# Two FFN chunks of batch 0 queued later, the first k and q of batch 1 and the transposes of batch 2 ahead of other loads

## The chip, the cores and the metric

The kernel runs on one core of a Trainium2 chip. The metric is the device time of one execution in microseconds (us); the median of several is compared. A core has a matrix engine (PE, with its weight loads listed as PEld), a vector engine (DVE), an engine for activation functions (ACT), a general one (POOL) and a synchronisation engine (SP). Each works through its own instructions in the order in which the program gives them. An instruction whose data is not there holds up all that stands behind it on its engine. Loads and stores are issued by POOL, SP or ACT and are then carried out by 16 DMA engines, while the issuing engine goes on.

## What is computed

Sigmoid attention for 8 batches of 12 heads, followed by a gated feed-forward network (FFN) over all 3584 tokens. All inputs are float32; the kernel converts them to float16 as it loads them.

```python
S = q.shape[2]                                   # 448; heads are 64 wide
scores = np.matmul(q, k.transpose(0, 1, 3, 2)) / sqrt(64) - np.log(S)
attn = 1.0 / (1.0 + np.exp(-scores))
x = np.matmul(attn, v)                           # then heads side by side: (3584, 768)
out = (np.maximum(x @ w_gate, 0) * (x @ w_val)) @ w_out   # 768 -> 1536 -> 768
```

## The kernel before

**The pieces.** A batch has 12 heads, worked in three groups of four (`NG = 3`; groups 0, 1, 2). For a group, k and q must first be transposed, so that the head dimension lies on partitions. For batches 0 and 1 PE does it (`pe_transposes`, L201: one call for k and one for q, into a PSUM tile `trt`, which DVE copies to `qkT`, L206). From batch 2 on DVE reorders k and q into `rel` (L215) and SP issues a DMA transpose (`dma_transposes`, L219). A group then has seven score units (`qk_unit`, L232: matmuls into two PSUM banks, then two sigmoids by ACT, L187), and after its seventh one product with v (`pv`, L250), whose result DVE scales into `xT` (L184).

**The FFN** works in 12 chunks of 128 columns of the gate and value weights. A chunk (`gv`, L309) is six matmuls for the gate into `g_ps` and six for the value into `v_ps`; then the gate's maximum with 0 by DVE (L320) or ACT (L318, where `act_relu` is true), and the product by DVE into `hT` (L327). Later batches, and batches 2 and 3 in part, use another form of the products with sums of weights (L393), which the change does not touch; `weight_sums` (L384) are DVE's sums over `wo` for it.

**Batch 0** is special. Its queries are cut in two halves of 256 and 192 (`HALVES`), and the work in six slots (`FirstSlot`: half by half, group by group) of four units each. A unit of two score chunks takes one of two double banks (`pairp`), so a third unit needs the sigmoid of the first. The table `after` says what PE does after unit u of slot i: transposes, products with v of earlier slots, or FFN chunks. Its FFN chunks come in two kinds: wide ones for the first half (256 columns) and narrow ones for the second (192), 12 of each.

**The FFN queue.** `push_first` and `push_gv` put chunks into `gv_queue`, and `ffn_mix(count, hooks)` takes `count` of them out, in order. A hook `(left, job)` runs its job when `left` chunks of the mix are still to come. Batch 1's scores come in six bursts of 3, 3, 3, 4, 4 and 4 units (`cuts`), and each burst is followed by a mix of so many chunks (`mix`). The hooks put into the mixes what must be ready for later bursts: PE transposes of batch 1's groups 1 and 2, and the DMA transposes of batch 2.

**The order of loads.** POOL issues all loads into one queue. Before anything else it has batch 0's k, q and v, the gate and value weights in pieces (`load_gv(f0, f1)`: chunks f0 to f1, the gate's piece `wg`, then the value's `wv`), and batch 1's k, q (by group) and v in between. The issues of k and q are L110, of v L114 and L116, of weights L148, of `wo` L164. In the first mix of batch 1 it gets batch 2's loads. `hold(b, g)` is a tiny POOL copy (L735) that reads a transposed tile: POOL, and so every load behind it, waits until that DMA transpose has landed. `late_loads` issues batch 2's last transposes, a hold, and the loads of `wo`; batch 3's k, q and v follow (they are issued in batch 2's first mix).

**PSUM banks.** During the slots four banks rotate (`ring0`) beside the two double banks. After the slots these become four more (`ring1`), and eight rotate (`bank`).

Of the kernel before, what the change touches and what calls it, by code (L numbers as in the profile page):

```python
# [17 lines left out]
def kernel(  # L18
# [84 lines left out]
    def rows_of(src, b):  # L103
        return src[b].rearrange("(x r) (t c) d -> (r t) x (c d)", r=2, c=NCH)

    def load(b, g0, g1, which, c0=0, c1=NCH):
        for nm, t16, src in zip("kq", tiles_of(b), (k, q)):
            if nm in which:
                xs, cs = slice(2 * g0, 2 * g1), slice(c0 * D, c1 * D)
                nc.gpsimd.dma_start(t16[:, xs, cs], rows_of(src, b)[:, xs, cs])  # L110

    def load_v(b):
        v16 = tiles_of(b)[2]
        nc.gpsimd.dma_start(v16[:, 0::2, :], rows_of(v, b)[:, 0::2, :])  # L114
        for r in range(2):
            nc.gpsimd.dma_start(  # L116
                v16[64 - 64 * r : P - 64 * r, 1::2, :], rows_of(v, b)[64 * r : 64 * r + 64, 1::2, :]
            )
# [25 lines left out]
    def load_gv(f0, f1, which=(0, 1)):  # L144
        fs = slice(f0 * P, f1 * P)
        for i in which:
            wt, src = ((wg, moe_w_gate), (wv, moe_w_val))[i]
            nc.gpsimd.dma_start(wt[:, :, fs], src[:, fs].rearrange("(c p) f -> p c f", p=P))  # L148
# [2 lines left out]
    load(0, 1, NG, "q", QCUT)  # L151
    load_gv(0, 2, (1,))
    load_gv(2, 4)
    load_gv(4, 6)
    load(1, 0, 1, "kq")
    load_gv(6, 9)
    load(1, 1, 2, "kq")
    load_v(1)
# [36 lines left out]
    def pe_transposes(b, g, ti, c0=0, c1=NCH):  # L195
        t16 = in_tiles[b][ti]
        qkT = qkT_of(b, g)
        trt = bank16("trt")
        for c in range(c0, c1):
            for h in range(2):  # L200
                nc.tensor.transpose(  # L201
                    trt[64 * h : 64 * h + 64, c * P : (c + 1) * P],
                    t16[:, 2 * g + h, c * D : (c + 1) * D],
                    ident[:],
                )
        nc.vector.tensor_copy(  # L206
            qkT[:, ti * NCH + c0 : ti * NCH + c1, :].rearrange("p c x -> p (c x)"),
            trt[:, c0 * P : c1 * P],
        )

    def dma_transposes(b, g):
        k16, q16, _ = in_tiles[b]
        rel = relp.tile([P, TW, P], FP16, tag="rel", name="rel")
        for ti, t16 in enumerate((k16, q16)):
            nc.vector.tensor_copy(  # L215
                rel[:, ti * NCH : (ti + 1) * NCH, :].rearrange("p c (h d) -> p h c d", h=2),
                t16[:, 2 * g : 2 * g + 2, :].rearrange("p h (c d) -> p h c d", c=NCH),
            )
        nc.sync.dma_start_transpose(  # L219
            qkT_of(b, g)[:], rel[:].rearrange("p c x -> p (c x)")  # L220
        )
# [433 lines left out]
    def push_first(half, fs, act_relu=True):  # L655
        c0, c1 = HALVES[half]
        push_gv(0, 64 * c0, 64 * (c1 - c0), fs, act_relu)

    def ffn_mix(count, hooks=()):
        hooks = list(hooks)  # L660
        for left in range(count, -1, -1):
            while hooks and hooks[0][0] >= left:
                hooks.pop(0)[1]()
            if left:
                gv_queue.popleft()()
# [8 lines left out]
    pe_transposes(0, 0, 1, 0, QCUT)  # L674
    keep_warm(2)
    slots = [FirstSlot(half * NG + g, g, half) for half in range(2) for g in range(NG)]
    push_first(0, range(0, 6), False)
    def second_queries():
        for g in range(1, NG):
            pe_transposes(0, g, 1, QCUT, NCH)  # L680

    def pv_then_ffn(i):
        slots[i].pv()
        ffn_mix(1)

    def ffn_then_pv(i):
        ffn_mix(1)
# [18 lines left out]
        (3, 3): lambda: ffn_mix(1),  # L706
        (4, 1): lambda: ffn_then_pv(3),
        (4, 3): lambda: ffn_mix(2),
        (5, 1): lambda: pv_then_ffn(4),
        (5, 3): lambda: ffn_mix(1),  # L710
    }
    for i, slot in enumerate(slots):
        for u in range(4):
# [1 line left out]
            if (i, u) in after:  # L715
                after[(i, u)]()
    slots[5].pv()
    push_first(1, range(0, 6))
    for f0 in range(6, 12, 2):
        for half in range(2):  # L720
            push_first(half, range(f0, f0 + 2))

# [11 lines left out]
    def hold(b, g):  # L734
        nc.gpsimd.tensor_copy(gate[0:1, :], qkT_tiles[(b, g)][0:1, 0, 0:2])  # L735

    def both(b, g):
        pe_transposes(b, g, 0)
        pe_transposes(b, g, 1)

    def late_loads():
        dma_transposes(2, 2)
        hold(2, 1)
        load_o()


# [38 lines left out]
            prepare()  # L785
            down(g, i)

    ffn_mix(1, [(1, lambda: both(1, 0))])
    for b in range(1, B):
        if b == 1:  # L790
            cuts, pv_at = (0, 3, 6, 9, 13, 17, 21), {3: (0, 2), 5: (1, 2)}
        else:
            cuts, pv_at = (0, 4, 7, 11, 14, 18, 21), {0: (-1, 2), 2: (0, 2), 4: (1, 2)}
        bursts = list(range(len(cuts) - 1))
        inner = {}
        if b > 2:
            inner = {0: 1} if b % 2 == 0 else {2: 3, 3: 5} if b == B - 1 else {4: 5}
            for n in inner.values():
                bursts.remove(n)
        count = len(bursts)  # L800
        hooks = {}
        if b == 1:
            mix = (3, 3, 3, 3, 3, 2)
            hooks = {
                1: [(1, lambda: both(1, 1))],
                3: [(1, lambda: both(1, 2))],
                4: [(3, lambda: dma_transposes(2, 0))],
                5: [(2, lambda: dma_transposes(2, 1)), (0, late_loads)],
            }
        elif b == 2:  # L810
            mix = (2, 2, 1, 1, 1, 2)
            hooks = {
                2: [(0, prepare)],
                4: [(0, lambda: weight_sums(0))],
                5: [(1, lambda: weight_sums(1)), (0, lambda: weight_sums(2))],
            }
            open_late()
        elif b == 3:
            mix = (1, 1, 1, 0, 0)
        else:  # L820
            mix = (0,) * count

        def burst(n):
            for i, (g, c) in enumerate(order[cuts[n] : cuts[n + 1]]):
                if n in pv_at and i == pv_at[n][1]:
                    if n == 0:
                        pv_finish(b - 1)
                        if b == 2:
                            push_group(0)
                        elif b % 2 == 0:  # L830
                            push_group(b // 2 - 1)
                    else:
                        pv_group(b, pv_at[n][0])
                qk_unit(b, g, c)

        if b == 3:
            dma_transposes(3, 2)
            for args in put_off:
                stored(*args)
        for m in range(count):  # L840
            jobs = []
            burst(bursts[m])
            if m == 0 and b > 3:
                jobs.append(lambda: dma_transposes(b, 2))
            if b == 2 and m == count - 1:
                jobs.append(lambda: (dma_transposes(3, 0), dma_transposes(3, 1)))
            elif b == 3 and m == count - 1:
                jobs.append(lambda: dma_transposes(4, 1))
            elif 0 <= m - count + 2 and 3 < b < B - 1:
                jobs.append(lambda: dma_transposes(b + 1, m - count + 2))  # L850
            if b == 1:
                if m == 0:
                    load(2, 0, 1, "kq")
                    load(2, 1, 2, "kq")
                    load(2, 2, 3, "kq")
                    load_v(2)
            elif m == 0 and b + 1 < B:
                if b == 3:
                    jobs.append(lambda: hold(3, 2))
                jobs.append(lambda: (load(b + 1, 0, 3, "kq"), load_v(b + 1)))  # L860
            if b % 2 and b > 2:
                if m == count - 1:
                    jobs.append(lambda: (batch_sums_t1(b // 2), batch_sums(b // 2, (0, 1))))
            elif b > 3 and m == 0:
                jobs.append(lambda: batch_sums(b // 2 - 1, (1, HD)))
            if b == 2 and m == count - 1:
                ffn_mix(mix[m], hooks[m])
                next_work(jobs + [lambda: weight_sums(3)], first_act=True)
            elif mix[m]:
                for job in jobs:  # L870
                    job()
                ffn_mix(mix[m], hooks.get(m, ()))
            else:
                next_work(jobs, amid=(lambda: burst(inner[m])) if m in inner else None)
            if b == 3 and m == count - 2:
                dma_transposes(4, 0)
            if b == 3 and m in (1, 3):
                for f in range(*((0, 8, 2), (8, NFC, 2))[m // 2]):
                    gate_sums(f, f + 2)
# [35 lines left out]
```

## Time and profile before

| | |
|---|---|
| median of three runs | 392.95 us (392.91 to 393.34) |
| the profiled execution | 392.75 us, of which 391.0 us from its first to its last instruction |
| granted TensorE clock | 0.998 |
| slots of batch 0 | up to about 31 us |
| bursts of batch 1 | 33.57 to 60.4 us, the first of batch 2 at 62.46 us |
| POOL held by batch 2's hold | until 67.76 us |
| read from HBM, written | 47.19 MB, 11.01 MB |

In the profile, L393 is line 393 of the code; `out<-in` gives the tiles that an instruction writes and reads. A line of a timeline has the start in us, the time from the first start to the last end of the instructions that it sums up, the engine, the line, the operation and how many there are; in brackets stands how long the engine was idle before it, and what ended that. Matmuls overlap, so two groups that follow each other closely can overlap by some 0.1 us on paper: the distance from start to start is what a group costs. An answer by tile lists instructions with their shortest, median and longest duration in ns, the start of the first and the last in us, and for loads the time from issue to landing.

### The profile page before, as it was taken

The numbers are of one execution on the slowest core, as the hardware profiler recorded it, in microseconds if no ns is written. First come the engines' busy times: TensorE is split into PE (matmuls) and PEld (weight loads), VectorE is DVE, ScalarE is ACT, GpSimd is POOL, SyncE is SP. The second block draws the span as 40 slices with busy tenths as digits, with TensorE's granted clock in tenths as the row PEclk, the third lists the DMA queues.
The fourth block names the chain that finished last, engine by engine and source line by source line (L and its number), as shares of the span: only waits on it lengthen the run. The fifth ranks groups of instructions, "written<-read, shape, count | busy, mean of one in ns | idle before, by whom it ended". The sixth has DMA issues, their size and how long they took to land.

```text
span 391.0 us, 8760 instructions
## 1 busy us (share of the span) xinstructions
PE 384.2 (98%) x3488; PEld 214.8 (55%) x3488; DVE 283.5 (73%) x557; ACT 226.9 (58%) x480; POOL 49.5 (13%) x73
## 2 busy tenths in 40 slices
PE   8999999999999999999999999999999999999996
PEld 3678786445455545454555554545455555555663
DVE  2454344358387789999757789999987788999663
ACT  5946778784777755555556774545467354333322
POOL 8633420500300300003000300000000000000000
PEclk9999999999999999999999999999999999999999
DMA  9999999998999892225956595132002320000335
GB/s 149 197 199 204 204 204 138 145 202 148 191 185 167 156 217 44 47 49 64 179 99 137 114 222 86 21 49 59 18 14 73 78 80 2 0 1 2 78 87 159
DMA packets 68953, 43.69 MB, mean 112 GB/s; under 512 B 35888, under 2 KB 65584, under 8 KB 68912
## 3 DMA queue, kind: packets, MB, share of 16 engines
q0 software_dynamic: 30736, 23.33, 39.8%
q1 hardware_dynamic: 37664, 19.24, 24.3%
q10 hardware_dynamic: 512, 0.56, 0.5%
q8 instruction: 27, 0.44, 0.5%
q14 instruction: 14, 0.11, 0.1%
HBM read 47.19 MB, written 11.01 MB: 149 GB/s over the span
## 4 chain that ended last, share of the span: by engine, by line
PE 90%; DMA 5%; POOL 1%; DVE 1%; ACT 1%; issue 0%; POOLq 0%; DVEq 0%; ACTq 0%
PE u L393 33%; PE g L393 16%; PE y L393 10%; PE qk_ps L232 8%; PE pv_ps L250 7%; PE g_ps L309 7%; PE v_ps L309 6%; DMA wv<-in_moe_w_val_dram 4%; DMA v<-in_v_dram 2%; PE ya L354 1%; PE trt L201 1%; PE yb L354 1%; POOL k L110 1%; POOL q L110 1%; ACT PT L187 1%
## 5 line engine op out<-in xcount | busy, mean ns | idle before, releaser
L187 ACT ACTIVATE PT<-qk_ps 128x448 f16<-128x448 f32 (+3 forms) x318 | 150.8, 585 | 76.2 <-PE qk_ps L232 76.1
L393 PEld LDWEIGHTS <-S 128*128 128x128 f16 x558 | 54.6, 98 | 44.7
L605 DVE TENSOR_TENSOR gsb<-g,gsb 128x448 f32<-128x448 f32 x72 | 42.8, 625 | 10.3 <-PE g L393 10.0
L232 PE MATMUL qk_ps<-qkT 64*64 64x448 f16 (+2 forms) x756 | 47.4, 335 | 0.8 <-DVE qkT L206 0.5
L327 DVE TENSOR_TENSOR hT<-gate_sb,v_ps 128x256 f16<-128x256 f32 (+2 forms) x36 | 16.2, 465 | 35.2 <-ACT gate_sb L318 18.0
L393 PEld LDWEIGHTS <-hT 128*128 128x128 f16 x306 | 28.7, 98 | 22.3 <-issue 4.9
L601 ACT COPY gsb<-u 128x448 f32<-128x448 f32 x48 | 25.6, 558 | 24.0 <-PE u L393 22.9
L445 ACT ACTIVATE ysb<-u 128x384 f32<-128x384 f32 x31 | 15.2, 491 | 38.2 <-PE u L393 33.8
L250 PE MATMUL pv_ps<-PT,v 64*64 64x448 f16 (+2 forms) x756 | 36.6, 329 | 0.0
L184 DVE TENSOR_SCALAR xT<-pv_ps 128x448 f16<-128x448 f32 (+2 forms) x53 | 27.9, 567 | 11.9 <-PE pv_ps L250 10.8
L309 PE MATMUL v_ps<-xT,wv 128*128 128x256 f16 (+2 forms) x216 | 33.3, 290 | 0.4 <-DMA wv<-in_moe_w_val_dram 0.4
L309 PE MATMUL g_ps<-xT,wg 128*128 128x256 f16 (+2 forms) x216 | 33.5, 291 | 0.1
L393 PEld LDWEIGHTS <-wg 128*128 128x128 f16 x216 | 20.2, 98 | 21.8 <-issue 4.3
L393 PEld LDWEIGHTS <-wv 128*128 128x128 f16 x216 | 21.1, 98 | 19.7
L232 PEld LDWEIGHTS <-qkT 64*64 64x64 f16 x756 | 17.9, 105 | 22.0 <-issue 14.7
L463 DVE SCALAR_TENSOR_TENSOR ysb<-y,ysb 128x384 f32<-128x384 f32 x29 | 16.1, 556 | 17.9 <-PE y L393 10.4
L250 PEld LDWEIGHTS <-v 64*64 64x64 f16 x756 | 21.7, 107 | 10.8 <-issue 0.9
L393 PE MATMUL u<-T,hT 128*128 128x384 f16 x132 | 25.1, 326 | 0.0
L110 POOL DMA_DIRECT2D k<-in_k_dram x14 | 10.9, 776 | 112.4 <-DVE rel L215 105.7
L309 PEld LDWEIGHTS <-wg 128*128 128x128 f16 x216 | 18.5, 98 | 11.7 <-issue 5.1
L309 PEld LDWEIGHTS <-wv 128*128 128x128 f16 x216 | 20.1, 98 | 8.1 <-DMA wv<-in_moe_w_val_dram 0.7
L393 PE MATMUL u<-xT,wg 128*128 128x448 f16 x108 | 23.5, 354 | 0.0
(76 smaller groups left out, 531.2 us busy)
## 6 DMA issues: line engine op xcount, KB each, us to landing
out_dram<-ysb SPq DMA_DIRECT2D x52, 192.0 KB, 2.8
k<-in_k_dram POOLq DMA_DIRECT2D x5, 672.0 KB, 11.4
q<-in_q_dram POOLq DMA_DIRECT2D x5, 672.0 KB, 14.7
v<-in_v_dram POOLq DMA_DIRECT2D x8, 336.0 KB, 14.9
v<-in_v_dram POOLq DMA_DIRECT2D x16, 168.0 KB, 13.8
k<-in_k_dram POOLq DMA_DIRECT2D x8, 224.0 KB, 11.9
wo<-in_moe_w_out_dram POOLq DMA_DIRECT2D x1, 1536.0 KB, 11.1
q<-in_q_dram POOLq DMA_DIRECT2D x6, 224.0 KB, 12.1
```

The lines of the kernel that those rows point to most:

```text
L110: nc.gpsimd.dma_start(t16[:, xs, cs], rows_of(src, b)[:, xs, cs])
L184: nc.vector.tensor_scalar(out=xT, in0=src, scalar1=XSCALE, scalar2=None, op0=AOP.mult)
L187: nc.scalar.activation(PT_ap, ps_ap, AF.Sigmoid, bias=sig_bias, scale=qk_scale)
L232: nc.tensor.matmul(out_of(hh)[o : o + 64, :], qkT[rows, c, cols], qkT[rows, NCH + c0 : NCH + c1, cols], start=True, stop=True, tile_positi ...
L250: nc.tensor.matmul(ps[hh][64 * r : 64 * r + 64, 0:qn], v16[rows, 2 * g + hh, c * D : (c + 1) * D], pieces[c][rows, hh, :], start=(c == 0), ...
L309: nc.tensor.matmul(ps[-1][:, 0:qn], wt[:, dc, f * P : (f + 1) * P], xT_tiles[b][:, dc, q0 : q0 + qn], start=(dc == 0), stop=(dc == NDC - 1),)
L327: nc.vector.tensor_tensor(out=hT_tiles[g][:, f, o : o + qn], in0=gate_sb[:, 0:qn], in1=ps[1][:, 0:qn], op=AOP.mult,)
L393: nc.tensor.matmul(ps[:, 0:n], A[:, k_, :], W[:, k_, :], start=(first and k_ == 0), stop=(k_ == kn - 1), skip_group_check=True,)
L445: nc.scalar.activation(o, ps[:, 0:HM], AF.Copy, scale=OUT_SCALE)
L463: nc.vector.scalar_tensor_tensor(out=o, in0=ps[:, 0:HM], scalar=OUT_SCALE, in1=o, op0=AOP.mult, op1=AOP.add)
L601: by(gs[u][i][:], ps[u][:, 0:S])
L605: nc.vector.tensor_tensor(out=gs[u][i][:], in0=ps[u][:, 0:S], in1=gs[u][i][:], op=AOP.add)
```

## The change

Four things change.

1. Batch 1's k and q of group 0 are issued ahead of the weights of chunks 4 and 5.
2. Chunks 4 and 5 of batch 0's first half leave the slots. They are now queued behind four narrow chunks, so that the order in the queue is 0 to 3 narrow, 4 and 5 wide, 4 and 5 narrow, 6 and 7 wide, and so on, where it was 0 to 5 narrow, 6 and 7 wide, 6 and 7 narrow, and so on. The queue has 20 chunks instead of 18. The two chunks get their gate by ACT and not by DVE.
3. Batch 1's first transposes go into slot 5, behind its third unit, and the single chunk between the slots and batch 1's first burst goes: the burst follows slot 5's product with v. The mixes of batch 1 become 4, 3, 3, 3, 3, 4, after one chunk ahead of them and 3, 3, 3, 3, 3, 2.
4. Batch 2's DMA transposes of group 1 go from the last mix of batch 1 into the fifth, with one chunk to come; those of group 2 go from the end of the last mix to behind its first chunk. POOL holds for group 2 instead of group 1, and batch 2's v is loaded behind that hold and ahead of `wo`; it was loaded ahead of the hold, behind batch 2's k and q.

```diff
@@ -151,8 +151,8 @@
     load_gv(2, 4)
+    load(1, 0, 1, "kq")
     load_gv(4, 6)
-    load(1, 0, 1, "kq")
     load_gv(6, 9)
@@ -674,14 +674,10 @@
-    push_first(0, range(0, 6), False)
+    push_first(0, range(0, 4), False)
...
-    def pv_then_ffn(i):
-        slots[i].pv()
-        ffn_mix(1)
@@ -706,8 +702,8 @@
-        (5, 1): lambda: pv_then_ffn(4),
-        (5, 3): lambda: ffn_mix(1),
+        (5, 1): slots[4].pv,
+        (5, 2): lambda: (pe_transposes(1, 0, 0), pe_transposes(1, 0, 1)),
@@ -715,8 +711,8 @@
     slots[5].pv()
-    push_first(1, range(0, 6))
-    for f0 in range(6, 12, 2):
+    push_first(1, range(0, 4))
+    for f0 in range(4, 12, 2):
@@ -740,7 +736,8 @@
     def late_loads():
         dma_transposes(2, 2)
-        hold(2, 1)
+        hold(2, 2)
+        load_v(2)
         load_o()
@@ -785,7 +782,6 @@
-    ffn_mix(1, [(1, lambda: both(1, 0))])
@@ -800,12 +796,12 @@
-            mix = (3, 3, 3, 3, 3, 2)
+            mix = (4, 3, 3, 3, 3, 4)
             hooks = {
                 1: [(1, lambda: both(1, 1))],
                 3: [(1, lambda: both(1, 2))],
-                4: [(3, lambda: dma_transposes(2, 0))],
-                5: [(2, lambda: dma_transposes(2, 1)), (0, late_loads)],
+                4: [(3, lambda: dma_transposes(2, 0)), (1, lambda: dma_transposes(2, 1))],
+                5: [(3, late_loads)],
             }
@@ -853,7 +849,6 @@
                     load(2, 2, 3, "kq")
-                    load_v(2)
```

## Prediction

> **What bounds the kernel now.** I read the page first, then TensorE's timeline (PE) of the first 110 us, the answers by tile for the loads, and last the DVE, ACT, POOL and SP timelines there.
>
> ```profile
> PE 384.2 (98%) x3488; PEld 214.8 (55%) x3488; DVE 283.5 (73%) x557; ACT 226.9 (58%) x480; POOL 49.5 (13%) x73
> DMA  9999999998999892225956595132002320000335
> GB/s 149 197 199 204 204 204 138 145 202 148 191 185 167 156 217 44 47 49 64 179 99 137 114 222 86 21 49 59 18 14 73 78 80 2 0 1 2 78 87 159
> ```
>
> PE is busy for 384.2 of 391.0 us, and the change takes no matmul away: it can only move PE's gaps. The rates say where a gap can arise: slices are 9.8 us, and until about 58 us the transfers run flat at some 200 GB/s, one queue, in the order written. In that stretch a load lands when the bytes ahead of it are through, however early PE wants it.
>
> ```profile
> 27.05 0.83 PE L309 MATMUL g_ps<-xT,wg 128*128 128x256 f16 x6
> 28.32 0.83 PE L309 MATMUL v_ps<-xT,wv 128*128 128x256 f16 x6 [0.45 <-DMA wv<-in_moe_w_val_dram]
> 38.03 0.67 PE L309 MATMUL g_ps<-xT,wg 128*128 128x192 f16 x6
> 38.53 0.66 PE L309 MATMUL v_ps<-xT,wv 128*128 128x192 f16 x6
> ...
> 40.53 0.56 PE L201 MATMUL trt<-ident,q 128*64 128x128 f16 x14
> ...
> 48.73 0.83 PE L309 MATMUL g_ps<-xT,wg 128*128 128x256 f16 x6
> 49.39 0.82 PE L309 MATMUL v_ps<-xT,wv 128*128 128x256 f16 x6
> ...
> 51.87 0.56 PE L201 MATMUL trt<-ident,q 128*64 128x128 f16 x14
> ```
>
> From start to start, half an FFN chunk costs 0.66 us when wide (256 columns, batch 0's first half) and 0.50 when narrow (192, the second half): 1.32 and 0.99 a chunk. The v half at 28.32 follows its g half by 1.27, so PE loses 0.61 there, waiting for the weights of chunk 4. The two transposes of q (L201) at 40.53 and 51.87 wait for nothing. How long had their data been there? POOL's loads of q for batch 1's groups 1 and 2:
>
> ```profile
> L110 POOL DMA_DIRECT2D q<-in_q_dram x1: 713/713/713, 23.9 to 23.9; - x1
> DMA to landing us min/median/max: 14.6/14.6/14.6
> ```
>
> ```profile
> L110 POOL DMA_DIRECT2D q<-in_q_dram x1: 713/713/713, 37.7 to 37.7; - x1
> DMA to landing us min/median/max: 12.3/12.3/12.3
> ```
>
> By POOL's timeline they start at 23.93 and 37.68, so they land at 38.5 and 50.0: 2.0 and 1.9 us before PE wants them. These two slacks decide the change.
>
> **The change, part by part.**
>
> *Loads.* Batch 1's first k and q (224 KB each, 1.1 us each in the stream) go ahead of the weights of chunks 4 and 5. They now land at 29.3 and 30.5; they will land near 24.8 and 25.9, and those weights at 30.5 instead of 28.3. Everything behind them lands when it did: the bytes ahead are the same.
>
> *Slot 5 and the first burst.* Out of the stretch from 26.0 go three FFN chunks, two wide and one narrow. With them go the 0.61 stall and three changes between FFN and scores, about 0.1 each (the v half before the scores of 29.08 takes 0.76, not 0.66). What comes in: slot 5's four sigmoids (1.51 and 1.19 us of ACT, now with PE's wait between) run on end, and PE has less to put beside them. Unit 2 needs unit 0's bank: ready at 26.48 + 0.76 and a hand-over, so 27.4, where PE arrives at 27.05; with some 0.15 before the last probabilities of the last pv, 0.5. Bounds: 0, if the transposes fill it, and 0.9, if the whole last pv and the burst stand behind ACT's end (26.48 + 2.70 + 0.70 + 0.69 = 30.6, against 29.7 of PE's own work from 26.0). The early balance is thus 0 to 0.9 us gained, likeliest 0.4. DVE's gate (0.42, L320) becomes ACT's (0.38, L318) for two chunks; ACT idles 4.8 of the 20 us from 34 to 54, so this costs nothing; without that room it would be 0.8.
>
> *The trap.* The moved chunks are work that stood ahead of the transposes and now stands behind them. At group 1's transposes PE has done two narrow chunks less than before (chunks 4 and 5 of the second half): it comes 4 x 0.50 = 2.0 earlier, besides the early gain. Slack 2.0: any early gain is waited away here, and PE leaves level with before. At group 2's it has done two wide chunks less (8 and 9 of the first half): 4 x 0.66 = 2.63 earlier, slack 51.87 - 49.98 = 1.89, and 0.05 from landing to start. **PE waits 0.79 us for q.** No later work returns it: the skipped chunks all come in mixes 4 and 5, and at batch 2's first burst PE has done the same as before, at 63.2 instead of 62.46. Bounds: 0.5 and 1.1, from one transfer's scatter in the same stream (a step of 1.12 or 1.15 us for 224 KB, but 2.7 for 384 KB where 1.9 is usual).
>
> *Batch 2's transposes.* Those of group 1 go up into mix 4 and of group 2 into mix 5 behind one chunk. Their six DVE copies (0.39 each) and SP's three transposes are the same. Group 2's copies stand behind the product of that chunk (about 60.6, since ACT ends eight sigmoids first), so SP issues it at about 61.7. It took 5.3 to 5.8 us there: group 2 lands at 66 to 67.5. Group 0's is needed at 63.2 and issued near 53; even at its 7.4 of now it is there.
>
> *v and wo.* POOL's hold moves from group 1 (released at 67.76) to group 2 (66 to 67.5), and behind it now stand three loads of v, two of wo, and batch 3's k, q and v. From hold to first issue is 1.1 us now (67.76 to 68.83); the wo that came first took 11.1 for 1536 KB, of which 9.4 is bytes at the rate of the second (768 KB in 4.7), so a start costs 1.7. v (672 KB, 3.4 us) then lands by 74; its first pv comes at 75.06 + 0.8 = 75.9. wo ends near 86 to 88, wanted by DVE at 87.61 + 0.8. Both costed at nothing, with 1 to 2 us of cover; without it, each microsecond late at v is one on PE. POOL gains 2.0 us of issues here; PE and DVE don't wait for POOL.
>
> *Batch 3's first transposes.* This is what is late next. Batch 3's v now lands last at 73.86 + 20.8 = 94.7, and SP starts group 0's transposes at 94.97, on empty queues; PE takes them up the moment they land:
>
> ```profile
> L219 SPq DMA_TRANSPOSE qkT<-rel x1: 1510/1510/1510, 95.0 to 95.0; - x1
> DMA to landing us min/median/max: 4.1/4.1/4.1
> ```
>
> ```profile
> 99.12 0.14 PEld L232 LDWEIGHTS <-qkT 64*64 64x64 f16 x8 [0.38 <-DMA qkT<-rel]
> ```
>
> After: v's 3.4 us more, less 0.2 to 1.8 from the earlier hold: the loads end at 96.3 to 97.9, SP starts at 95.77. So they overlap by 0.5 to 2.1. What overlap costs:
>
> ```profile
> L219 SPq DMA_TRANSPOSE qkT<-rel x1: 3106/3106/3106, 54.7 to 54.7; - x1
> DMA to landing us min/median/max: 7.4/7.4/7.4
> ```
>
> That one had 5.9 us of loads beside it (until 60.55) and took 3.3 longer, 0.56 per us. This gives 0.3 to 1.2; I take 0.5, since its data moves only about 1 us after the issue. Bounds: nothing (the loads are out first) and 1.6 (SP's issue alone went from 1.51 to 3.11).
>
> The Trainium skill ("DMA: Bandwidth & Descriptors", Queues, rings and completion order) says that each DMA engine goes round between the queues that have work, packet by packet. That both queues move at once is what the row of 54.7 shows too. By the rule a transpose beside a load gets half of each engine and is held up by half of the true overlap: an estimate from that page of 0 to 0.5 us, and a sum of 393.54 to 394.04. The row is a little dearer, and the sum stays with the row.
>
> The skill also has a rule that speaks for the change: "Mode switching requires drain" ("TensorEngine Tiling (Array Packing)", Key Properties). It names no price; the trace agrees with about 0.1 us each. By the rule the early stretch gains three of them, and the sum is the same, since the gain is waited away at group 1's transposes.
>
> **Sum.** The profiled execution took 392.75 us (span 391.0 and 1.75 around it): 392.75 + 0 (early gain, lost) + 0.79 (q of group 2) + 0.5 (batch 3's transposes) = 394.05. The median shown is 392.95, 0.2 above that execution, so I forecast **394.2**. A change under 0.2% (0.79 us) can't be told from none here.
>
> **Rivals.**
> 1. *The q is late and nothing else*, or late by less: 392.95 + 0 to 0.79, up to 393.74. For it: batch 3's loads may end before SP's data moves. Against: the stall at 99.12 shows no cover there.
> 2. *v or wo takes over.* v is late if the hold is released after 69.4 (75.9 less 1.1, 1.7, 3.4 and 0.3). Group 2's landing is 63.75 + 5.3 = 69.06 now, for a copy 2 us later in the program, so this is near. Price 1 to 3 us: 395.3 to 397.
> 3. *Faster.* The loads keep pace: q of group 2 must land by 49.2 (0.8 earlier) and of group 1 at 38.1. Then the 0.61 stall and the switches are saved: 0.4 to 0.8, so 392.15 to 392.5. It decides only if those landings move; against it speak the flat 200 GB/s and unchanged bytes ahead of both. A stream 2% faster would do it for group 2.
>
> **Chances.** The forecast (q late, batch 3's transposes somewhat late, 393.5 to 395.3) 0.62; rival 1: 0.16; rival 2: 0.12; rival 3: 0.10. Above 393.74 lie most of the forecast (0.58) and rival 2: slower 0.70. Within 0.2%: rival 1 and 0.04 of the forecast, 0.20. Faster 0.10. The range 392.9 to 395.9 leaves out rival 3 and the far end of rival 2.
>
> **What would show it.** The 0.61 stall at chunk 4's v half is gone. PE waits for DMA q at group 1's transposes (about 38.5) and 0.8 us at group 2's (about 50.0), both named. Batch 2's first burst starts near 63.2, hold ends at 66 to 67.5, v lands before 75, and the wait at batch 3's first scores has grown to 0.5 to 1.5 over 0.38. The prediction is wrong if q of group 2 lands before 49.3, if pv of batch 2 waits for v, or if PE makes up time between 63 and 99 us.

## The result and the profile after

| | before | after |
|---|---|---|
| median of 21 runs each | 393.09 us (392.46 to 394.21) | 393.97 us (393.47 to 395.11) |
| the profiled execution | 392.75 us, span 391.0 | 394.54 us, span 392.7 |

The ratio is 1.0022, with a 95% interval of 1.0016 to 1.0029: **0.88 us slower**. The profiled execution of after lies 0.57 above its median, and that of before 0.34 below its own, so the two traces differ by 1.8 us where the kernels differ by 0.9. What is not typical is named below. Bursts and mixes of batch 1 are numbered from 0 to 5 here, as in the code.

The page of the changed kernel, its busy time of engines and its transfers in 40 slices:

```profile
PE 385.2 (98%) x3488; PEld 215.8 (55%) x3488; DVE 282.4 (72%) x555; ACT 227.8 (58%) x482; POOL 49.4 (13%) x73
...
DMA  9999995998999793224956595042103320000335
GB/s 152 198 199 205 203 176 93 195 203 149 198 173 172 143 214 66 47 48 48 170 107 142 114 216 99 12 52 56 26 7 76 82 80 2 0 1 2 78 88 157
```

The stream still runs at 200 GB/s until batch 2's k and q are in. The slices from 49 to 69 us have become emptier (176 and 93 for 204 and 138), since v now waits for the hold. PE's timeline of the changed kernel, in the stretch that the change rewrites:

```profile
27.47 0.36 PE L232 MATMUL qk_ps<-qkT 64*64 64x192 f16 x8 [0.23 <-ACT PT L187]
...
28.86 0.33 PE L201 MATMUL trt<-ident,q 128*64 128x128 f16 x5 [0.24 <-issue]
...
30.05 0.28 PE L250 MATMUL pv_ps<-PT,v 64*64 64x192 f16 x4 [0.16 <-ACT PT L187]
...
38.72 0.56 PE L201 MATMUL trt<-ident,q 128*64 128x128 f16 x14
...
49.00 0.58 PE L201 MATMUL trt<-ident,k 128*64 128x128 f16 x14
49.81 0.58 PE L201 MATMUL trt<-ident,q 128*64 128x128 f16 x14 [0.23 <-DMA q<-in_q_dram]
...
56.14 0.79 PE L232 MATMUL qk_ps<-qkT 64*64 64x448 f16 x8
56.56 1.77 PE L250 MATMUL pv_ps<-PT,v 64*64 64x448 f16 x28
57.98 0.72 PE L232 MATMUL qk_ps<-qkT 64*64 64x448 f16 x8
58.63 0.83 PE L309 MATMUL g_ps<-xT,wg 128*128 128x256 f16 x6
...
63.34 0.57 PE L232 MATMUL qk_ps<-qkT 64*64 64x448 f16 x8
```

Chunk 4's stall on its weights is gone. In its place stand two short waits for ACT in slot 5, a wait for q at group 2's transposes, and a burst 5 whose pieces take longer on paper (before, its pv took 1.49). The wait at 49.81 is longer than its bracket, because the transposes of k beside it are drawn overlapping: k's start at 49.00 and cost 0.42 before, so PE was free at 49.42 and lost 0.39. The load of that q, by its answer by tile:

```profile
L110 POOL DMA_DIRECT2D q<-in_q_dram x1: 713/713/713, 36.8 to 36.8; - x1
...
DMA to landing us min/median/max: 13.0/13.0/13.0
```

It lands at 49.77 (before: 49.98), and PE starts at 49.81.

To see where time comes in, I set both traces' PE instructions of the same work side by side; from batch 2's first burst on their order is the same. The changed kernel is behind by 0.12 us when the two programs first differ (at 26.0; scatter of the first loads), by 0.18 at the first chunk after batch 1's first burst, by 0.61 after group 2's transposes, by 0.88 at batch 2's first burst (63.34 against 62.46), and still by 0.86 at batch 3's first scores. That is close to the difference of the medians. The trace then loses another 0.79 at 121.9, which belongs to this execution:

```profile
118.95 0.39 DVE L215 COPY rel<-q 128x896 f16<-128x896 f16 x1 [1.22 <-DMA q<-in_q_dram]
...
121.86 1.14 PE L393 MATMUL u<-T,S 128*128 128x384 f16 x6 [0.63 <-DVE ysb L440]
```

DVE waits for batch 4's q, whose load took 12.6 us here and 11.3 before. None of the nine experiments' traces has this step.

### The profile page after: what moved, and what is told of

Read it like the earlier page. It is cut to its first block, busy times and chain, and to the rows that moved or that the text cites. A ratio compares the mean times of both kernels' runs of the same rounds, so it can differ in the third digit from the quotient of the medians.

```text
span 392.7 us, 8755 instructions
## 1 busy us (share of the span) xinstructions
PE 385.2 (98%) x3488; PEld 215.8 (55%) x3488; DVE 282.4 (72%) x555; ACT 227.8 (58%) x482; POOL 49.4 (13%) x73
## 4 chain that ended last, share of the span: by engine, by line
PE 81%; DMA 13%; POOL 2%; DVE 2%; issue 1%; ACT 0%; POOLq 0%; DVEq 0%; ACTq 0%
PE u L393 33%; PE g L393 16%; PE y L393 10%; PE qk_ps L232 7%; DMA q<-in_q_dram 7%; PE pv_ps L250 6%; PE g_ps L309 4%; PE v_ps L309 4%; DMA k<-in_k_dram 4%; DMA wg<-in_moe_w_gate_dram 3%; POOL q L110 1%; PE ya L354 1%; POOL k L110 1%; ACT PT L187 0%; PE yb L354 0%
```

## The experiments

The theory at the start: the loss is the wait for q at group 2, and the part on batch 2 costs nothing. The rivals: the late v and wo cost it, or slot 5 under ACT's pace does. Times are medians; "before" is run beside each group (393.05, 393.19 and 392.95).

| run | us | ratio to before, 95% interval |
|---|---|---|
| e1_front_only | 394.26 | 1.0040 (1.0028 to 1.0052) |
| e2_back_only | 393.18 | 1.0008 (0.9999 to 1.0017) |
| e3_q_early | 393.59 | 1.0015 (1.0006 to 1.0023) |
| e4_mix | 393.98 | 1.0020 (1.0008 to 1.0032) |
| e5_dve_gate | 393.41 (one run) | |
| e6_both_q | 392.89 | 0.9996 (0.9988 to 1.0005) |
| e7_fill | 392.77 | 0.9993 (0.9983 to 1.0003) |
| e8_back_no_v | 392.94 (one run) | |
| e9_fill_again | 392.73 | 0.9994 (0.9984 to 1.0004) |

### The change without its part on batch 2 (e1_front_only)

```diff
     def late_loads():
         dma_transposes(2, 2)
-        hold(2, 2)
-        load_v(2)
+        hold(2, 1)
         load_o()
...
-                4: [(3, lambda: dma_transposes(2, 0)), (1, lambda: dma_transposes(2, 1))],
-                5: [(3, late_loads)],
+                4: [(3, lambda: dma_transposes(2, 0))],
+                5: [(2, lambda: dma_transposes(2, 1)), (0, late_loads)],
...
+                    load_v(2)
```

> The change without its part on batch 2: transposes, hold and the load of v stand as before the change. Theory (the loss is PE's wait for q of batch 1's group 2, and the part on batch 2 costs nothing): as the changed kernel, 0.7 to 1.0 us above the kernel before (about 394.0), and PE still reaches that q about 0.4 us too soon. Rival (v and wo behind the later hold cost the time): within 0.2 us of the kernel before.

It is 1.2 us above before, more than the expected 0.7 to 1.0, so the front part holds all of the loss. The rival falls. Its PE timeline at the two groups' transposes:

```profile
38.55 0.58 PE L201 MATMUL trt<-ident,q 128*64 128x128 f16 x14 [0.20 <-DMA q<-in_q_dram]
...
48.90 0.58 PE L201 MATMUL trt<-ident,k 128*64 128x128 f16 x14
50.34 0.58 PE L201 MATMUL trt<-ident,q 128*64 128x128 f16 x14 [0.86 <-DMA q<-in_q_dram]
```

PE lost 0.36 at group 1 (k's start there is 37.77) and 1.02 at group 2 (k's start plus 0.42, up to q's start). The place is right; the expected 0.4 was the size of one execution. The stream's landings scatter: this q landed at 50.29.

### Only the part on batch 2 (e2_back_only)

```diff
-        hold(2, 1)
+        hold(2, 2)
+        load_v(2)
...
-                5: [(2, lambda: dma_transposes(2, 1)), (0, late_loads)],
+                5: [(1, late_loads)],
```

with group 1's transposes in mix 4 and v gone from its old place, as in the change.

> Only the part on batch 2, on the kernel before: transposes of groups 1 and 2 earlier, hold for group 2, v behind it and ahead of wo. Theory: within 0.2 us of the kernel before (about 393.1), v lands over 1 us before its first pv. Rival (this part costs the time): 0.6 to 1.0 us above it.

Time says 0.13 us, within the theory's 0.2, but its trace corrects it. Up to batch 2's first burst it is 0.25 us ahead of the trace of before, only because chunk 4's weights came in time here. At batch 3's first scores, by its PEld timeline, it loses 0.58:

```profile
99.45 0.14 PEld L232 LDWEIGHTS <-qkT 64*64 64x64 f16 x8 [0.96 <-DMA qkT<-rel]
```

These are the transposes that the prediction called late next. SP's answer by tile:

```profile
L219 SPq DMA_TRANSPOSE qkT<-rel x1: 2224/2224/2224, 94.7 to 94.7; - x1
...
DMA to landing us min/median/max: 4.7/4.7/4.7
```

Issue 2.22 instead of 1.51, landing after 4.7 instead of 4.1, with the loads of batch 3's v still running until 97.46 (94.66 before). In the changed kernel the loads ended at 95.94, SP started at 95.83, and this cost nothing.

### Group 2's q ahead of the weights (e3_q_early)

```diff
     load_v(1)
-    load_gv(9, 12)
     load(1, 2, 3, "kq")
+    load_gv(9, 12)
```

> The changed kernel, but batch 1's k and q of group 2 are loaded ahead of the weights of chunks 9 to 11. They then land near 43 and 44 us, and those weights near 50, where chunk 9 is wanted at about 52.5. Theory: PE's wait for q at about 49.8 is gone, and the kernel is 0.4 us faster than the changed one: 0.4 to 0.6 above the kernel before. Rival (the loss sits in slot 5, which ACT paces, and the wait only stands in for it): as the changed kernel, 0.8 to 1.0 above.

0.54 us above before, within the theory's 0.4 to 0.6. Its PE timeline:

```profile
38.71 0.58 PE L201 MATMUL trt<-ident,q 128*64 128x128 f16 x14 [0.52 <-DMA q<-in_q_dram]
...
49.44 0.56 PE L201 MATMUL trt<-ident,q 128*64 128x128 f16 x14
```

No wait at group 2. But PE now waits at group 1 (0.68: free at 38.03): this execution gained 0.40 in slot 5 and gave it all away there. So the two slacks stand one behind the other, and repairing the second alone leaves the first.

### FFN work moved ahead of group 2's transposes (e4_mix)

```diff
-            mix = (4, 3, 3, 3, 3, 4)
+            mix = (4, 3, 4, 4, 3, 2)
...
-                5: [(3, late_loads)],
+                5: [(1, late_loads)],
```

> The changed kernel with mixes 4, 3, 4, 4, 3, 2 instead of 4, 3, 3, 3, 3, 4, and batch 2's last transposes one chunk before the end: PE has done as much FFN before group 2's transposes as in the kernel before, and comes to them 2.6 us later than in the changed kernel. Theory: no wait for q, 0.4 us faster than the changed kernel, 0.4 to 0.6 above the kernel before. Rival (slot 5 alone): as the changed kernel, 0.8 to 1.0 above.

0.93 us above before. That is the rival's number, but the trace shows other reasons. In it slot 5 gains 0.40, there is no wait at either group, and burst 5 takes its old 2.21 us; relative to its own start it is 0.41 ahead of before at batch 2's first burst (it started slot 5 0.54 late, which is scatter of the first loads). Then it loses 0.64 at batch 3's first scores, by its PEld timeline:

```profile
99.89 0.14 PEld L232 LDWEIGHTS <-qkT 64*64 64x64 f16 x8 [1.02 <-DMA qkT<-rel]
```

Its hold was released at 68.27, and batch 3's v landed at 97.95. The expectation had left this out. Apart from the late start these steps come to only 0.23 us over before (0.64 less 0.41); what else the median's 0.93 holds doesn't show in this one trace, and stays open.

### Burst 5 and ACT's queue (e5_dve_gate)

In all three kernels so far that have the changed mixes, burst 5 takes 2.49 or 2.50 us, and 2.21 in those that don't. In the changed kernel, ACT and DVE show why:

```profile
55.58 0.91 ACT L318 ACTIVATE gate_sb<-g_ps 128x256 f32<-128x256 f32 x3
56.07 0.69 DVE L327 TENSOR_TENSOR hT<-gate_sb,v_ps 128x256 f16<-128x256 f32 x2 [3.13 <-ACT gate_sb L318]
```

Eight banks rotate, and three chunks and a unit use them up, so the burst's second unit takes the banks of chunk 9, the first chunk after burst 4. That chunk's gate waits for ACT to end eight sigmoids, its product (0.42) for the gate: free at 56.49, and the unit goes on at 56.55. Before, mix 4 had two wide chunks and one narrow (3.70 us) and burst 5 came later; now it has one wide and two narrow (3.38). The same place in the kernel before (DVE's products of mix 4, then burst 5 and the chunk behind it), from its DVE and PE timelines:

```profile
57.73 1.04 DVE L327 TENSOR_TENSOR hT<-gate_sb,v_ps 128x192 f16<-128x192 f32 x3 [3.14 <-ACT gate_sb L318]
...
58.17 0.57 PE L232 MATMUL qk_ps<-qkT 64*64 64x448 f16 x8
...
60.38 0.67 PE L309 MATMUL g_ps<-xT,wg 128*128 128x192 f16 x6
```

There the first chunk after burst 4 was a narrow one, its gate on ACT too. Its product ended at 58.08 (57.73 + 0.35), in time for the second unit at 58.38.

```diff
-            push_first(half, range(f0, f0 + 2))
+            push_first(half, range(f0, f0 + 2), (f0, half) != (8, 0))
```

> The changed kernel, but the gates of chunks 8 and 9 of batch 0's first half come from DVE and not from ACT. In the changed kernel burst 5 of batch 1 takes 2.49 us to the next chunk, before the change 2.21: its second unit starts when DVE's product for chunk 9 ends (56.49), and that product stands behind ACT's eight sigmoids. Theory (the bank is held by ACT's queue): burst 5 takes 2.21 again. Rival (the packed matmuls run unevenly for another reason, such as the DMA transposes beside them): 2.49 again. The whole is 0.3 us, too small for one execution's time.

The PE timeline of this kernel, against 56.14 to 58.63 above:

```profile
56.03 0.57 PE L232 MATMUL qk_ps<-qkT 64*64 64x448 f16 x8
56.43 1.49 PE L250 MATMUL pv_ps<-PT,v 64*64 64x448 f16 x28
57.75 0.55 PE L232 MATMUL qk_ps<-qkT 64*64 64x448 f16 x8
58.23 0.83 PE L309 MATMUL g_ps<-xT,wg 128*128 128x256 f16 x6
```

2.20 us: the theory holds, although the DMA transposes run beside it as before. In the traces of e6, e7 and e9, which have these gates too, it is 2.21. Group 2's q cost 0.74 in this execution (k's start at 48.54 plus 0.42, up to 49.70).

### The repairs together (e6_both_q)

```diff
-    load_gv(6, 9)
     load(1, 1, 2, "kq")
+    load_gv(6, 9)
     load_v(1)
-    load_gv(9, 12)
     load(1, 2, 3, "kq")
+    load_gv(9, 12)
```

with DVE's gates of the experiment above.

> The changed kernel with batch 1's k and q of group 1 ahead of the weights of chunks 6 to 8, those of group 2 ahead of the weights of chunks 9 to 11, and the gates of chunks 8 and 9 by DVE. Theory (the change gains 0.4 us in slot 5 and gives it back at late q and in burst 5): no wait for q at either group, burst 5 at 2.21, and 0.3 to 0.5 us faster than the kernel before: 392.5 to 392.8. Rival (slot 5 gains nothing, since the stall that it removes is not there in most executions): 0 to 0.3 us above the kernel before.

0.30 us below before, at the lower end of the theory, and 1.1 below the changed kernel. The intervals of the two against before don't meet; that of e6 holds no difference too. Its PE timeline has no DMA wait left at either group:

```profile
38.45 0.56 PE L201 MATMUL trt<-ident,q 128*64 128x128 f16 x14
...
49.15 0.56 PE L201 MATMUL trt<-ident,q 128*64 128x128 f16 x14
```

### A chunk moved into slot 5 (e7_fill, e9_fill_again)

```diff
-        (4, 3): lambda: ffn_mix(2),
-        (5, 1): slots[4].pv,
+        (4, 3): lambda: ffn_mix(1),
+        (5, 1): lambda: (slots[4].pv(), ffn_mix(1)),
```

> As e6_both_q, and the second of the two FFN chunks after slot 4's last unit moves behind slot 4's product with v in slot 5, where PE waits for ACT. Slot 5 to the first chunk takes 4.23 us of which some 3.7 are work. Theory (ACT paces the slot): the waits of 0.3 before unit 2 and 0.16 in the last product with v go, and it is 0.2 to 0.4 us faster than e6_both_q. Rival (PE is held there by something else): same as e6_both_q.

> e7_fill unchanged, to tell whether it is faster than the kernel before: its interval of 0.9983 to 1.0003 holds both. Theory (0.4 gained in slot 5 and 0.2 by the chunk moved into it, nothing given back): 0.3 to 0.6 us below the kernel before, ratio 0.9985 to 0.9993. Rival (the gain is the weights' stall, which differs from execution to execution): within 0.2 us of it.

The two runs give 0.42 and 0.22 us below before; each interval just reaches 1. The second lies between its theory (0.3 to 0.6) and its rival (within 0.2), and the first is only 0.12 below e6, less than the 0.2 to 0.4 expected. So it beats the changed kernel, and its lead over the kernel before, some 0.3 us, is likely and not shown. In the traces, slot 5 up to the first chunk costs 4.03 and 4.02 us besides the FFN in it, against 4.23 of the plain change: ACT's pace was worth 0.2, the lower end of what was expected. The wait before unit 2 is gone; one in the last product with v stays.

### Batch 2's transposes moved, v not (e8_back_no_v)

```diff
     def late_loads():
         dma_transposes(2, 2)
         hold(2, 2)
-        load_v(2)
         load_o()
...
+                    load_v(2)
```

against e2_back_only.

> As e2_back_only, but batch 2's v is loaded where it was before the change: only the transposes and the hold move. In e2_back_only batch 3's v landed last at 97.46, after the start of batch 3's first transposes at 94.72, and PE lost 0.58 us at batch 3's first scores. Theory (the v behind the hold pushes batch 3's loads into those transposes): the loads end near 94, and the loss at batch 3's first scores is gone. Rival (the moved hold or transposes cause it): still 0.5 to 0.6.

The loads end at 94.91, before SP's start at 95.03, and the loss is gone (the step there is under 0.05 us). The PEld timeline at batch 3's first scores, as before the change:

```profile
99.14 0.14 PEld L232 LDWEIGHTS <-qkT 64*64 64x64 f16 x8 [0.34 <-DMA qkT<-rel]
```

So it is v behind the hold, not the moved hold, that can reach batch 3's first transposes. The landing of the last load alone doesn't decide it. In e9 that came at 96.50, 1.8 us after SP's start at 94.69, and yet SP took 1.51 to issue, the transpose landed after 4.1, and PE lost nothing:

```profile
98.83 0.14 PEld L232 LDWEIGHTS <-qkT 64*64 64x64 f16 x8 [0.38 <-DMA qkT<-rel]
```

There the loads had thinned out: from 95.0 to 95.5 they moved 36 GB/s, where e2 still had 197.

## Why the prediction held, step by step

- **What bounds the kernel**: held. PE's work is the same, and only its gaps move.
- **Slot 5** ("0 to 0.9 us gained, likeliest 0.4"): right in size, but not in every execution. From slot 5's start to the first chunk after batch 1's first burst, less the FFN in it, the six traces with the change's slot take 4.23 or 4.24 (e3, e4, e5), 4.33 (e1), 4.48 (e6) and 4.68 (the changed kernel); the three with the slot of before take 4.01 (e2), 4.63 (before) and 4.85 (e8). The latter lose 0, 0.61 and 0.83 to chunk 4's weights. So the change swaps a stall of 0 to 0.8 for a net 0.22 of ACT's pace. Against the trace of before it gains 0.4 three times, and in the changed kernel's own trace it loses 0.05. That trace had a further hold-up in the transposes of q: 0.45 by the distance from q's start to the scores behind it (0.94, and 0.49 in e5), of which the bracket shows 0.24. e6 had 0.25 and e1 0.1 of it, always behind the ninth of the fourteen transposes. Nothing in the traces names its cause, and it stays open.
- **The trap at group 1** ("any early gain is waited away here"): right where there was a gain and q was no earlier (0.36 in e1, 0.68 in e3). In the changed kernel's trace slot 5 had gained nothing, and this q landed at 37.58, 0.9 earlier than before, so PE didn't wait. In e5 it waited only 0.06, with q there at 38.19. Group 2 then took what was left.
- **The trap at group 2** (0.79): the mechanism is shown by e3 and e6, where earlier loads take the wait away, and by e4, where later transposes do. Measured 0.39, 1.02 and 0.74 in the three executions that have it, 0.72 on average. What counts is how far PE is behind the trace of before when it leaves group 2: 0.61, 1.13 and 0.49, on average 0.74. q's landing sets this, whatever slot 5 gained.
- **DVE's gates to ACT, "this costs nothing"**: held for the two chunks that it speaks of, 4 and 5. Bursts 2, 3 and 4 behind them cost PE 0.70, 2.21 and 1.02 us, and 0.69, 2.21 and 1.02 before; ACT itself was idle for 0.59 ahead of burst 4's sigmoids.
- **Left out: burst 5** (0.28). The prediction followed the chunks that change places ("the skipped chunks all come in mixes 4 and 5"; chunk 8 comes behind the transposes in mix 3 already, which changes nothing in the sum) and took the burst behind mix 4 as unchanged. Chunk 9's gate was ACT's before, too. But now this wide chunk opens mix 4, and the mix is 0.32 shorter. Before, the bank was free 0.30 ahead of the unit, which leaves 0.25 after a hand-over of 0.06; 0.32 less time, 0.05 more for the gate and 0.07 more for the product make it 0.19 late, which is the wait in the trace. It takes both: e4 has the gates on ACT and the old mix 4, e5 the new mix and the gates of chunks 8 and 9 on DVE, and in both burst 5 is back at 2.2.
- **v and wo**: right. The hold ended at 66.17 (forecast 66 to 67.5), v landed at 73.15 (by 74), its pv came at 75.93; wo landed at 85.85 (forecast 86 to 88), and DVE took it up at 88.47.
- **Batch 3's transposes** (0.5): nothing in the changed kernel, whose loads ended 0.4 us ahead of the forecast's earliest, because POOL took 0.48 and not 1.1 us from the hold to the next issue. The cost is real where the hold is released 1.6 to 2.1 us later and v stands behind it: 0.58 in e2, 0.64 in e4, but none in e8, where v doesn't. For this place the price was set too high: 0.56 per us of overlap came from one row at 54.7, and here e2 and e4 lost 0.58 and 0.64 for 2.7 and 2.9 us, some 0.2 per us.

The sum had 0.79 + 0.5 (which gives 394.04 and not 394.05); the forecast of 394.2 lay 1.25 above the median then known, and 0.88 were measured. The trace has 0.39 (q) + 0.28 (burst 5) and 0.2 of scatter and slot 5. So the mechanism of the main term is shown, but that the total came near is partly luck: one term was halved in this execution, one didn't come, and 0.28 that had been overlooked made up for part of them.

## What to carry to other kernels

While a load queue runs full, work that is moved behind a consumer brings that consumer forward; subtract the landing from its old start, and move no more than this slack. Where a queue item takes a buffer that a busy engine must first empty, price it by what is queued ahead of it there when the buffer is next wanted, and do so again when the work in between gets shorter. A gain ahead of a late load isn't a gain until the load moves too: here the loads had to be reordered before PE stopped waiting, and the lead that was left, some 0.3 us, isn't clear of the noise.

## What the runs showed of the hardware

- Four packed 64x64 matmuls that run in step lost it when one of them waited. Before, the four starts lay within 0.01 us; after a wait of 0.2 us in burst 5's second unit they spread over some 0.1, the 28 matmuls of pv spanned 1.77 us instead of 1.49, the next eight 0.72 instead of 0.55, and the burst cost 0.28 more.
- In one order of loads the same q landed between 49.65 and 50.29 us in four executions (the changed kernel, e1, e4, e5), and chunk 4's weights cost PE 0, 0.61 and 0.83 in three others: a gap that one trace shows can be worth nothing in the next.
- A DMA transpose beside a running load stream took longer to issue, and not only to move its data: 1.51 us alone, 2.22 in e2 and 2.34 in e4 at batch 3, 3.11 before the change at 54.7. It is no fixed price: at 53 to 55 us it ranged from 1.64 (e4) to 4.15 (e1), and beside the thin end of the stream in e9 it was 1.51.
